# Agent attention with a top-1 mixture of experts: another path for the second phase's left rows, and earlier checks in the last batch

## The chip, the cores and the metric

The kernel runs on one core of one Trainium2 chip. The metric is the device time of one execution in microseconds. Three runs of the kernel before took 730.01, 725.21 and 724.99 us, a median of 725.21 us.

## The reference

Four batches of 11456 tokens with 128 channels pass an attention through 49 agents, and the rows that come out pass a mixture of 8 experts, of which each row takes the one with the largest logit.

```python
a2k = sm(agents, k)                 # softmax over the tokens
agent_v = a2k @ v
x = sm(q, agents) @ agent_v         # 45824 rows of 128
e_idx = argmax(x @ w_gate)
h = maximum(x[mask] @ w1[e], 0)     # for each expert e, mask = rows that chose e
out[mask] = gate_w * eom * (h @ w2[e])
```

`gate_w` is the softmax probability of the chosen expert and `eom` the sigmoid of its output gate.

## The kernel before

For each batch the kernel averages `v` under the agents' weights and takes the expert that this average favours, the "dominant" one. Nearly all rows choose it, so the main stream computes all rows of a batch with that expert's weights, folded down to the agents. Each batch has 12 units of up to 1024 tokens (90 columns of 128 in all); a unit has two tiles of up to 512 columns, which `mm1` (line 1521) and `mm2` (1547) multiply.

A unit of queries goes through `q_rest` (1306: maximum and difference on VectorE, into a tile `ef` of a ring of FRONT = 6), `weights` (1321: exponentials, then the transposed copy `x1`, which stands in one of 13 places: 7 LARGE, which also take the loads of q, k and v, and 6 SMALL), `route` (1347) and `gate` (1374: the gate values, and a store of `ef` to a table in HBM). The list `rests` notes for each unit how far it is: 1 with `x1` there, 2 within `gate`, 3 with `ef` stored. `roomy` (1299) lets the units of the last batch run 9 ahead of the main stream. `gate` spawns `signs` (1428) at priority 1: for each of the 90 columns one matmul `ck` and one ScalarE activation `cx` whose sum tells whether the fold could be wrong for a row. When all units are checked, `q_tail` (1452) makes on VectorE a table of 128 x 8 x 90 running counts of the rows that must be computed again, the "left rows", stores it, and writes its totals to `tot`.

The left rows are collected by expert into tiles of 128, in two phases: batches 0 and 1 have 14 tiles, batches 2 and 3 have 4 (`PHASES`, line 38). `left_prepare` (1947) waits until the phase's batches are counted and the phase before is prepared, and runs

- `left_table` (1665): which expert and which ranks belong to which tile;
- `left_index` (1736) for each set of tiles (phase 0: 4, 4, 4 and 2 tiles, whose names end in 0s, 4s, 8s and 12s; phase 1: one set of 4): which partition and which column of it holds each row, by comparisons on VectorE, one gather per tile from the counts (`big<-cumd`), some fifteen small steps, and one gather per tile from the stored exponentials (`big<-efd`), all gathers on GpSimd's queue. The set 12s starts only when 8 tiles are stored.

`left_static` (1975) then computes the 18 tiles in order: `left_load` (1863) fetches the expert's two matrices, 512 KB each, into one of two homes (`lw` and `lws` in the trace), `left_front` (1894) rebuilds the rows (`let`, `lx`), `left_back` (1911) multiplies them by both matrices (`lh`, then `ly`, 8 matmuls in four-byte numbers each), and `left_scatter` (2008) writes the rows out through GpSimd's queue. Homes are loaded again only when the tile that used them is done.

No order is written out by hand. All these parts are Python generators; `spawn(generator, priority)` hands them to a planner (`tick`, 527, and `Clock`, 67) that keeps a modelled time of every engine and emits an instruction when its operands should be ready, lower priority numbers first. TensorE's stream has slots for them between the main matmuls. Every engine works its queue in the order of emission, so an instruction that was emitted too early holds up what stands behind it. Nearly all instructions are recorded in one helper, so their line in the profile is 248; they are told apart by tile.

Of the kernel before, what the change touches and what calls it, by code (L numbers as in the profile page):

```python
# [17 lines left out]
P = 128  # L18
B, N, C, A, E, F = 4, 11456, 128, 49, 8, 1024
A2 = 50  # L20
# [38 lines left out]
K_W = K_GA2 + NG_  # L59
# [238 lines left out]
def agent_attention_top1_moe(ctx, tc, qT, kT, v, aT, wg, wo, w1, w2, cst, sides, slots, out):  # L298
# [95 lines left out]
    ticol = kc[:, K_TI:K_TI + 2]  # L394
    own = kc[:, K_OWN:K_OWN + 1]
# [45 lines left out]
    ls = cp.tile([2 * E, P + 2], F32, name="ls")  # L441
# [170 lines left out]
    def place(item, k, shape, dt=F32):  # L612
        kind, b, u = item
        t = ld.tile([P] + shape, dt, name=f"{kind}{b}_{u}_ld", tag=f"ld{k}", bufs=1)
        places[k] = [False, t.name]
        held[item] = k
        return t
# [27 lines left out]

    def loads():
        for n, item in enumerate(ITEMS):
            while n >= FIRST_ITEMS and (picking[0] or not X1):
                yield None
            while not vacant():  # L650
                yield None
            yield from load(item)
            if n == 1:
                load_constants()

# [640 lines left out]
    rests = []  # L1296
    squared = set()
# [8 lines left out]
    def q_rest(b, u, s, mark):  # L1306
        base, pp, nt = UNITS[u]
        me = len(rests)
        rests.append(0)
        while me >= FRONT and rests[me - FRONT] < 3 or me > 1 and not state.get(0, {}).get("w"):  # L1310
            yield None
        sv = s[0:pp, 0:nt * A2].rearrange("p (t a) -> p t a", a=A2)[:, :, 0:A]
        m = wk.tile([P, 8], F32, name=f"qm{b}_{u}", tag="qm", bufs=3)
        yield from DVE.q.tensor_reduce(m[0:pp, 0:nt], sv, axis=AX.X, op=ALU.max)
        ef = wk.tile([P, 8, A2], F32, name=f"ef{b}_{u}", tag="ef", bufs=FRONT)
        ev = ef[0:pp, 0:nt, 0:A]
        yield from DVE.q.tensor_tensor(ev, sv, m[0:pp, 0:nt].unsqueeze(2).broadcast_to([pp, nt, A]), op=ALU.subtract)
        release(mark)
        spawn(weights(b, u, me, ef, ev), 1)

    def weights(b, u, me, ef, ev):
# [23 lines left out]
        spawn(route(b, u, me, x1, ef), 0.3)  # L1345

# [27 lines left out]
    def gate(b, u, me, x1, ef, L, lm, d256, rr, tl):  # L1374
# [9 lines left out]
        vs = vss[b % 2][:, 8 * u:8 * u + nt]  # L1384
        spawn(signs(b, u, me, x1, vs), 1)
# [37 lines left out]
        if u == NU - 1:  # L1423
            spawn(q_tail(b), 0.5)
# [26 lines left out]

    def q_tail(b):

        while NU * b + NU - 1 not in signed or "thr" not in state[b]:
            yield None
        e2, dq, vs = e2s[b % 2], dqs[b % 2], vss[b % 2]
        yield from DVE.q.scalar_tensor_tensor(e2, e2, state[b]["thr"], dq, op0=ALU.mult, op1=ALU.is_gt)
        yield from DVE.q.scalar_tensor_tensor(e2, vs, 0.0, e2, op0=ALU.is_gt, op1=ALU.max)
        c0 = wk.tile([P, E, NCOL], F32, name=f"cum{b}", tag="cum", bufs=1)
        f = c0.rearrange("p e t -> p t e")  # L1460
        yield from DVE.q.tensor_tensor(f, e2.unsqueeze(2).broadcast_to([P, NCOL, E]),
                                       state[b]["ndom"].unsqueeze(1).broadcast_to([P, NCOL, E]), op=ALU.max)
        yield from DVE.q.tensor_tensor(f, f, oht[b % 2], op=ALU.mult)
# [192 lines left out]
    lp = ctx.enter_context(tc.tile_pool(name="lp", bufs=1))  # L1656
    NSTM = max(x[2] for x in PHASES)
# [7 lines left out]
    def left_table(ph):  # L1665
# [30 lines left out]
        ppt = lt(f"pptsb{ph}", [P], f"_{ph}", [P])  # L1696
# [165 lines left out]

    def left_load(ph, ti, k, nm, home=None):
# [4 lines left out]
        if home == "sel":  # L1868
# [78 lines left out]
    def left_prepare(ph):  # L1947
# [4 lines left out]
        if ph == 0:  # L1952
            yield from SY.q.dma_start(ls, sides)
        yield from left_table(ph)
# [20 lines left out]
    def left_static():  # L1975
# [5 lines left out]
        def fronts():  # L1981
            for i, (ph, k) in enumerate(todo):
                while (ph, k) not in known or i > finished[0] + 1 or busy["own"] and (busy["sel"] or planning()):
                    yield None
                home = "sel" if busy["own"] else "own"
                busy[home] = True
                w1t, w2t = yield from left_load(ph, *known[ph, k], f"{ph}_{k}", home)
# [8 lines left out]

        spawn(fronts(), 0.3)
# [40 lines left out]
    spawn(loads(), -1)  # L2038
    spawn(gate_norm(), 5)
# [34 lines left out]
def _consts():  # L2074
# [8 lines left out]
    k[:, K_TI:K_TI + 2] = i[:, None] + 128 * np.arange(2)  # L2083
    k[:, K_OWN] = i < 2 * A
# [7 lines left out]
def _sides():  # L2092
# [3 lines left out]
    return np.concatenate([sign * (np.arange(P)[None] + 0.5), g % E, sign], axis=1).astype(np.float32)  # L2096
# [36 lines left out]
```

## Time and profile before

| what | us |
|---|---|
| median of three runs | 725.21 |
| profiled execution, its own time | 728.79 |
| its span, first to last instruction | 727.0 |
| TensorE busy in the span | 641.8 |
| VectorE, ScalarE, GpSimd busy | 506.2, 498.1, 277.3 |

The profiled execution is 1.8 us longer than its span and 3.6 us longer than the median. Instants below are microseconds from the start of the span. TensorE's mean granted clock is 0.973 of full speed. A row of the timeline gives start, duration, engine, operation, output and inputs; in brackets stands how long the engine was idle before it and what released it.

### The profile page before, as it was taken

Reading aid. Unit: us, or ns where it says so; the run is one execution under the profiler, and the core shown is the slowest. Engines: PE = TensorE matmul, PEld = TensorE weight load, DVE = VectorE, ACT = ScalarE, POOL = GpSimd, SP = SyncE. Lnnn points to the kernel's source line nnn. Section 1 sums busy time; section 2 is a strip of 40 time slices with the busy share of each in tenths; the row PEclk is TensorE's granted clock in tenths of the full one; section 3 lists DMA queues with packets and bytes.
Section 4 is the critical chain, followed back from the end, with each engine's and each line's share of the span. In section 5 each row is a group of like instructions: output and inputs, shape, how many; then the busy total and the mean of one; then the engine's idle time right before and its main releaser. Section 6 shows DMA issues by size and latency. Waiting matters only on the chain. (4 is left out here: it accounts for less than half of the span.)

```text
span 727.0 us, 27442 instructions
## 1 busy us (share of the span) xinstructions
PE 641.8 (88%) x10693; PEld 533.2 (73%) x10693; DVE 506.2 (70%) x1744; ACT 498.1 (69%) x1724; POOL 277.3 (38%) x569
## 2 busy tenths in 40 slices
PE   9998989898998898799999888969999999996174
PEld 7788877687775787588777577858887789786064
DVE  1677868786878965789888889777687866544300
ACT  2325568996878886687888789666788878772021
POOL 2011247822132677223257623433455354122231
PEclk9999999999999999999999999999999999999678
DMA  8788697799566579976759995536563743455221
GB/s 304 279 250 276 194 272 257 220 224 285 167 187 195 145 230 307 270 220 164 223 157 286 255 259 162 151 96 197 144 196 114 206 163 135 163 182 150 97 76 58
DMA packets 103110, 143.81 MB, mean 198 GB/s; under 512 B 60188, under 2 KB 68541, under 8 KB 102976
## 3 DMA queue, kind: packets, MB, share of 16 engines
q1 hardware_dynamic: 101248, 139.95, 65.0%
q0 software_dynamic: 1728, 2.06, 1.3%
q8 instruction: 85, 1.39, 0.8%
q14 instruction: 49, 0.40, 0.2%
HBM read 95.23 MB, written 35.43 MB: 180 GB/s over the span
## 5 line engine op out<-in xcount | busy, mean ns | idle before, releaser
L248 PE MATMUL y<-vv,hh 128*128 128x128 f16 (+1 forms) x1440 | 159.5, 220 | 1.7 <-issue 1.7
L248 ACT ACTIVATE cx<-ck 128x256 f16<-128x256 f32 x360 | 139.6, 388 | 26.2 <-PE ck L248 20.5
L248 PE MATMUL y<-vv,hl 128*128 128x128 f16 x720 | 139.8, 220 | 0.0
L248 DVE SCALAR_TENSOR_TENSOR hl<-h,hh 128x512 f16<-128x512 f32 (+1 forms) x184 | 117.9, 669 | 17.9 <-ACT hh L248 16.1
L248 PEld LDWEIGHTS <-x_ld 128*128 128x128 f16 (+1 forms) x1440 | 97.9, 99 | 41.7 <-issue 24.0
L248 PEld LDWEIGHTS <-hh 128*128 128x128 f16 (+1 forms) x1440 | 113.8, 99 | 6.6 <-issue 3.2
L248 ACT ACTIVATE hh<-h 128x512 f16<-128x512 f32 (+1 forms) x184 | 101.5, 591 | 15.1 <-PE h L248 14.4
L248 PE MATMUL y<-gw,x_ld 128*128 128x128 f16 x720 | 79.8, 220 | 4.4 <-ACT cx L248 2.2
L248 PE MATMUL ck<-wc,x_ld 128*128 128x256 f16 x360 | 72.6, 274 | 7.3 <-ACT cx L248 2.7
L248 PEld LDWEIGHTS <-hl 128*128 128x128 f16 x720 | 73.5, 102 | 2.9 <-issue 1.6
L248 ACT ACTIVATION_READ_ACCUMULATOR cx<-ck 128x1 f32 x360 | 74.5, 207 | 0.0
L248 PE MATMUL h<-x_ld,w 128*128 128x512 f16 (+1 forms) x184 | 69.1, 376 | 4.9 <-DMA x_ld<-e 3.4
L248 DVE TENSOR_TENSOR os<-y,smt 128x256 f32<-128x256 f32 (+1 forms) x92 | 38.1, 414 | 49.1 <-ACT os L248 43.5
L248 POOL TENSOR_TENSOR e<-ef,e 128x392 f16<-128x392 f32 (+1 forms) x48 | 43.1, 898 | 69.5 <-ACT e L248 68.6
L248 PE MATMUL h<-x_ld,wr 128*128 128x512 f16 (+1 forms) x184 | 68.6, 373 | 0.0
L248 ACT ACTIVATE os<-y,smt 128x128 f32<-128x128 f32 x180 | 56.7, 367 | 11.4 <-PE y L248 9.5
L248 PE MATMUL warm<-apart 128*128 128x256 f16 (+1 forms) x286 | 47.6, 290 | 11.7 <-DVE hl L248 3.8
L248 PE MATMUL ks<-at,k_ld 128*32 128x50 f32 (+1 forms) x2024 | 51.7, 218 | 3.0 <-issue 3.0
L248 PEld LDWEIGHTS ks<-at,k_ld 128*32 128x32 f32 (+1 forms) x2024 | 43.9, 123 | 12.3 <-issue 5.7
L248 PEld LDWEIGHTS <-apart 128*128 128x128 f16 x382 | 40.7, 123 | 15.6 <-issue 9.0
L248 ACT COPY S<-ks 128x400 f32<-128x400 f32 (+1 forms) x48 | 22.5, 469 | 38.8 <-PE ks L248 38.5
L248 PE MATMUL qs<-at,q_ld 128*32 128x50 f32 (+1 forms) x2504 | 46.8, 211 | 2.2 <-ACT hgc L248 1.1
(345 smaller groups left out, 1477.2 us busy)
## 6 DMA issues: line engine op xcount, KB each, us to landing
v_ld<-v SPq DMA_DIRECT2D x44, 512.0 KB
q_ld<-qT SPq DMA_DIRECT2D x44, 512.0 KB
out<-os SPq DMA_DIRECT2D x88, 256.0 KB
k_ld<-kT SPq DMA_DIRECT2D x43, 512.0 KB
lw<-w SPq DMA_DIRECT2D x18, 512.0 KB
lws<-w SPq DMA_DIRECT2D x18, 512.0 KB
efd<-ef SPq DMA_DIRECT2D x44, 200.0 KB
w1t<-w SPq DMA_DIRECT2D x4, 512.0 KB
```

The source lines that it names most:

```text
L248: return getattr(self.eng, op)(*a, **k)
```

## The change

Last batch: its units may run 12 ahead of the main stream instead of 9; an `ef` that finds no room in the ring takes a LARGE place, as long as three stay free while loads are still to come; `signs` is spawned in `weights`, right behind the transposed copy, at priority 0.25 instead of 1 and no longer in `gate`; and `q_tail` treats columns 0 to 79 when the first ten units are through and the other ten columns after that, with one scan over all at the end.

Second phase: `left_table` and `left_index` give way to `late_table`, `late_index` and `late_end`. The tables are read as sums of steps (a comparison, a product and a sum over nine), rows are compared in PSUM without a copy to SBUF, the gathers of the four tiles are worked on one by one, and the tables that only the overflow loop reads are made last. `late_weights` fetches the matrices of the four tiles as soon as the experts are known, into free LARGE places, and into the two old homes once phase 0 is done. The table of partition sums has one buffer for both phases. A few columns of constants are added, and four small memsets at the start.

```diff
-        while me >= FRONT and rests[me - FRONT] < 3 or me > 1 and not state.get(0, {}).get("w"):
-            yield None
+        while me > 1 and not state.get(0, {}).get("w"):
+            yield None
+        while True:
+            if len(fronts_) < FRONT or rests[fronts_[-FRONT]] > 2:
+                at_ = None
+                break
+            at_ = first_place(0, LARGE, 0 if loaded[0] else 3) if b == B - 1 else None
+            if at_ is not None:
+                break
+            yield None
+            fronts_.append(me)
+            ef = wk.tile([P, 8, A2], F32, name=f"ef{b}_{u}", tag="ef", bufs=FRONT)
+        else:
+            ef = place(("ef", b, u), at_[1], [1024])[:, 0:8 * A2].rearrange("p (t a) -> p t a", a=A2)
...
+        if b == B - 1:
+            spawn(signs(b, u, me, x1, vss[b % 2][:, 8 * u:8 * u + nt]), 0.25)
...
-        vs = vss[b % 2][:, 8 * u:8 * u + nt]
-        spawn(signs(b, u, me, x1, vs), 1)
+        if b < B - 1:
+            spawn(signs(b, u, me, x1, vss[b % 2][:, 8 * u:8 * u + nt]), 1)
...
-        if u == NU - 1:
+        if ("ef", b, u) in held:
+            scored(("ef", b, u))
+        if u == (CUT // 8 if b == B - 1 else NU) - 1:
             spawn(q_tail(b), 0.5)
...
+    CUT = 80
...
-        while NU * b + NU - 1 not in signed or "thr" not in state[b]:
-            yield None
...
+        c0 = None
+        for lo, hi in ((0, CUT), (CUT, NCOL)) if b == B - 1 else ((0, NCOL),):
+            us = range(NU if hi == NCOL else CUT // 8)
+            while not all(NU * b + u in signed and rests[NU * b + u:NU * b + u + 1] == [3] for u in us) or "thr" not in state[b]:
+                yield None
+            if c0 is None:
...
+            yield from DVE.q.tensor_tensor(f, e2.unsqueeze(2).broadcast_to([P, hi - lo, E]),
...
+            yield from DVE.q.tensor_tensor(f, f, oht[b % 2][:, lo:hi], op=ALU.mult)
...
-            while kind == "q" and not roomy(NU * b + u, 9 if b == B - 1 else AHEAD):
+            while kind == "q" and not roomy(NU * b + u, 12 if b == B - 1 else AHEAD):
...
+    def left_steps(n9, W, first, step, prod, o):
...
+        yield from DVE.q.tensor_tensor(step, n9.unsqueeze(1).broadcast_to([P, n, 9]),
+                                       first.unsqueeze(2).broadcast_to([P, n, 9]), op=ALU.is_le)
+        yield from DVE.q.tensor_tensor(prod, step.unsqueeze(2).broadcast_to([P, n, 4, 9]),
+                                       W.unsqueeze(1).broadcast_to([P, n, 4, 9]), op=ALU.mult)
+        yield from DVE.q.tensor_reduce(o, prod, axis=AX.X, op=ALU.add)
+
+    def late_table(ph, big):
...
+        yield from PE.q.matmul(cn_[:, 0:ng], ones, tt_, start=True, stop=True)
+        yield from DVE.q.tensor_copy(c10[:, 0, 1:9], cn_[:, 0:E])
+        yield from DVE.q.tensor_tensor(c10[:, 1, 1:9], cn_[:, E:2 * E], c10[:, 0, 1:9], op=ALU.add)
+        release(mark)
+        ti_ = lt("t1i", [E], f"_{ph}", [E], I32)
+        yield from DVE.q.tensor_scalar(ti_, c10[:, 1, 1:9], 127.0, None, op0=ALU.add)
+        yield from DVE.q.tensor_scalar(ti_, ti_, -128, None, op0=ALU.bitwise_and)
+        yield from DVE.q.tensor_copy(W[:, 3, 1:9], ti_)
+        yield from DVE.q.tensor_tensor(W[:, 1:3, :], c10[:, :, 1:10], c10[:, :, 0:9], op=ALU.subtract)
+        yield from DVE.q.tensor_tensor_scan(n9[:, 1:9], ones[:, 0:E], W[:, 3, 1:9], 0.0, op0=ALU.mult, op1=ALU.add)
+        yield from DVE.q.tensor_tensor(W[:, 1:3, :], W[:, 1:3, :], W[:, 3, :].unsqueeze(1).broadcast_to([P, 2, 9]), op=ALU.add)
...
+        PE.matmul(pt_[0:ng, 0:P], tt_, tri, start=True, stop=False)
+        PE.matmul(pt_[0:ng, 0:P], tt_, idf, start=False, stop=True)
...
+        yield from ACT.q.copy(ppt[0:ng], pt_[0:ng, 0:P])
...
+        yield from left_steps(n9, W, kc[:, K_KK:K_KK + n], big[:, 0:9 * n].rearrange("p (n e) -> p n e", e=9),
...
+        yield from DVE.q.tensor_scalar(nd, tb[0:ng, :, 0], expert, BIG, op0=ALU.not_equal, op1=ALU.mult)
+        yield from DVE.q.scalar_tensor_tensor(low, tb[0:ng, :, 1], sign, ls[:, P + 2:P + 2 + n], op0=ALU.mult, op1=ALU.subtract)
+        yield from DVE.q.tensor_tensor(nd, nd, low, op=ALU.add)
...
+        yield from DVE.q.tensor_scalar(ti, tb[:, :, 0], float(E - 1), None, op0=ALU.min)
...
+    def left_places(nm, n, tb, rk, bi, r, base, b2):
...
+        yield from DVE.q.tensor_tensor(bi[:, :, 1:3], rk.unsqueeze(2).broadcast_to([P, n, 2]), tb[:, :, 1:3], op=ALU.is_ge)
+        yield from DVE.q.tensor_tensor(r, rk, start, op=ALU.subtract)
...
+        yield from DVE.q.tensor_scalar(bi[:, :, 0], bt, -1.0, 1.0, op0=ALU.mult, op1=ALU.add)
...
+    def late_end(ph):
...
+        yield from left_steps(n9, W, ticol8, f[:, 0:9 * kr].rearrange("p (n e) -> p n e", e=9),
...
+        yield from POOL.q.memset(tt, 0.0)
...
+    def late_index(ph, nm, big, oa_, got):
...
+        yield from DVE.q.tensor_tensor(c[0:ng], side.unsqueeze(1).broadcast_to([ng, n, P]),
+                                       nd.unsqueeze(2).broadcast_to([ng, n, P]), op=ALU.is_ge)
...
+        for k in range(n):
+            yield from PE.q.matmul(t[:, k * P:(k + 1) * P], c[0:ng, k, :], ppt[0:ng], start=True, stop=True)
...
+        yield from left_places(nm, n, tb, kc[:, K_RK:K_RK + n], bi, r, base, b2)
...
+        yield from DVE.q.tensor_tensor(c, pb, r.unsqueeze(2).broadcast_to([P, n, P]), op=ALU.is_le)
+        pst = col("pst")
+        yield from DVE.q.tensor_reduce(pst, c, axis=AX.X, op=ALU.add)
+        ru = col("ru", U32)
+        yield from DVE.q.tensor_tensor(ru, pst, base, op=ALU.add)
...
+        for k in range(2):
+            yield from gather(k)
+        yield from DVE.q.tensor_tensor(c, c, pb, op=ALU.mult)
+        yield from DVE.q.tensor_reduce(ppx, c, axis=AX.X, op=ALU.max)
...
+        yield from DVE.q.memset(ef, 0.0)
+        yield from DVE.q.scalar_tensor_tensor(b2, pst, 8.0, b2, op0=ALU.mult, op1=ALU.add)
+        for k in range(n):
+            if k + 2 < n:
+                yield from gather(k + 2)
+            yield from pause(landed[k] + 200.0 - clk.now())
+            s_, x = slice(k, k + 1), cr[:, k:k + 1, :]
+            yield from DVE.q.tensor_scalar(x[:, 0], x[:, 0], ppx[:, s_], None, op0=ALU.is_le)
+            yield from DVE.q.tensor_reduce(c7[:, s_], x[:, :, 7:NCOL:8], axis=AX.X, op=ALU.add)
+            yield from DVE.q.scalar_tensor_tensor(f[:, s_], x[:, :, 87], -6.0, pst[:, s_], op0=ALU.mult, op1=ALU.mult)
+            yield from DVE.q.tensor_reduce(cc[:, s_], x, axis=AX.X, op=ALU.add)
+            yield from DVE.q.tensor_tensor(f[:, s_], f[:, s_], b2[:, s_], op=ALU.add)
...
+            yield from DVE.q.tensor_tensor(tu[:, s_], f[:, s_], cc[:, s_], op=ALU.add)
+            yield "POOL", [tu], [], 0
+            POOL.indirect_dma_start(out=ef[:, k, :], out_offset=None, in_=efd[ph],
...
+            got(k, clk.ready[big.name] + 200.0, None, tu, tg, ef, oa, xt, two)
+            yield from DVE.q.scalar_tensor_tensor(tg[:, s_], f[:, s_], float(b0 * N), cc[:, s_], op0=ALU.add, op1=ALU.add)
...
+        if home not in (None, "own", "sel"):
+            w1t, w2t = (place((*home, j), first_place(0, LARGE)[1], [F]) for j in range(2))
...
+        if ph == len(PHASES) - 1:
+            while sum(x[0] for x in places[:LARGE]) < 2:
...
+            big, oa_ = (place((x, ph, 0), first_place(0, LARGE)[1], [1024]) for x in ("lb", "lo"))
+            yield from late_table(ph, big)
+            averaged[ph] = yield from left_averages(ph, f"{ph}")
...
+            yield from late_index(ph, f"s{ph}_0", big, oa_, got)
+            yield from late_end(ph)
+            prepared[0] = ph + 1
+            return
...
-                while (ph, k) not in known or i > finished[0] + 1 or busy["own"] and (busy["sel"] or planning()):
+                while (ph, k) not in known or i > finished[0] + 1 or ph < last_ and busy["own"] and (busy["sel"] or planning()):
+                    yield None
+                while ph == last_ and (ph, k) not in weights_:
                     yield None
...
+                if (ph, k) in weights_:
+                    home, w1t, w2t = weights_.pop((ph, k))
...
+        def late_weights():
+            for k in range(PHASES[last_][2]):
+                while (last_, k) not in known:
+                    yield None
+                while True:
+                    if len([j for j in range(LARGE) if places[j][0]]) > 1:
+                        home = ("left", last_, k)
+                    elif finished[0] >= len(todo) - PHASES[last_][2] and not (busy["own"] and busy["sel"]):
+                        home = "sel" if busy["own"] else "own"
+                    else:
+                        yield None
+                        continue
```

## Rows read from the trace of the kernel before

**Rows 1.** Stretches: busy PE, PEld, DVE, ACT, POOL (instructions), clock, DMA share, GB/s

```profile
600.00:620.00 20.00, 20.00 (x234) 17.97 (x234) 12.36 (x59) 15.85 (x64) 9.05 (x21) 1.00 0.43 146
...
680.00:700.00 20.00, 5.52 (x23) 4.96 (x24) 4.25 (x20) 1.55 (x4) 8.06 (x9) 0.50 0.07 13
700.00:727.00 27.00, 15.30 (x119) 14.20 (x118) 0.00 (x0) 6.27 (x17) 3.97 (x4) 0.88 0.26 87
```

**Rows 2.** Timeline, the four tiles of phase 1 to the last instruction

```profile
693.77 0.42 PE L248 MATMUL let<-kc,big 128*98 128x128 f32 x1 [19.26 <-DVE big L248]
...
695.70 3.78 PE L248 MATMUL lh<-lxs,lw 128*128 128x128 f32 x16 [0.35 <-ACT lxs L248]
...
708.46 2.05 PE L248 MATMUL lh<-lxs,lw 128*128 128x128 f32 x16 [0.35 <-ACT lxs L248]
...
713.03 2.05 PE L248 MATMUL lh<-lxs,lws 128*128 128x128 f32 x16 [0.39 <-ACT lxs L248]
...
717.67 0.98 POOL L248 DMA_INDIRECT out<-big,ltg_0s  x1 [2.33 <-ACT big L248]
```

**Rows 3.** Timeline, phase 1's table and index from the counts to the first tile

```profile
656.80 0.40 PE L248 MATMUL pexc<-tot,kc 128*128 128x16 f32 x2 [1.48 <-DVE tot L248]
...
665.15 0.17 DVE L248 TENSOR_REDUCE tt<-cm 128x2 f32<-128x16 f32 x1 [3.44 <-POOL tt L248]
...
668.56 0.19 DVE L248 COPY tbs<-tbs 128x32 f32<-128x32 f32 x1 [1.22 <-PE tbs L248]
...
674.55 0.59 ACT L248 COPY big<-pbs 128x512 f32<-128x512 f32 x1 [0.27 <-PE pbs L248]
...
675.16 0.69 DVE L248 TENSOR_TENSOR big<-big,lrs 128x512 f32<-128x512 f32 x1 [3.91 <-ACT big L248]
...
678.73 0.17 DVE L248 CAST lrus<-lrgs 128x4 uint32<-128x4 f32 x1
679.68 1.05 POOL L248 DMA_INDIRECT big<-cumd,lrus  x1 [4.15 <-issue]
...
683.66 1.00 POOL L248 DMA_INDIRECT big<-cumd,lrus  x1 [0.30 <-issue]
...
686.97 0.53 DVE L248 TENSOR_TENSOR big<-big,lppxs 128x360 f32<-128x360 f32 x1 [8.07 <-DMA big<-cumd,lrus]
...
690.38 0.17 DVE L248 CAST ltg_0s<-lts 128x4 uint32<-128x4 f32 x1
690.89 1.00 POOL L248 DMA_INDIRECT big<-efd,ltu_0s  x1 [5.95 <-issue]
...
693.40 0.26 DVE L248 TENSOR_TENSOR big<-big,ltwo_0s 128x98 f32<-128x98 f32 x1 [2.85 <-DMA big<-efd,ltu_0s]
```

**Rows 4.** Timeline, phase 0's last set, `q_tail`'s scan and phase 0's last tiles

```profile
643.14 1.00 POOL L248 DMA_INDIRECT big<-cumd,lrus  x1 [0.30 <-issue]
...
648.18 0.34 DVE L248 TENSOR_TENSOR big<-big,lppxs 128x180 f32<-128x180 f32 x1
...
648.63 2.05 PE L248 MATMUL lh<-lxs,lw 128*128 128x128 f32 x16 [0.57 <-ACT lxs L248]
...
653.90 1.65 DVE L248 TENSOR_TENSOR_SCAN cum<-apart,cum 128x720 f32<-128x720 f16 x1
...
656.50 0.17 DVE L248 CAST ltu_12s<-lts 128x2 uint32<-128x2 f32 x1
...
668.82 2.05 PE L248 MATMUL lh<-lxs,lws 128*128 128x128 f32 x16 [0.30 <-ACT lxs L248]
...
674.55 0.98 POOL L248 DMA_INDIRECT out<-big,ltu_12s  x1 [4.67 <-DMA lw<-w]
```

**Rows 5.** The checks' ScalarE work (tile `cx`, two instructions a check) in two stretches

```profile
600.00:620.00 20.00, 7.64 (x32) 1.00 0.43 146
...
640.00:660.00 20.00, 5.69 (x24) 1.00 0.56 166
```

**Rows 6.** Timeline of SyncE's queue, the last unit's store of `ef`

```profile
623.67 0.33 SPq L248 DMA_DIRECT2D efd<-ef  x1
```

More of the change, by code (lines that the diff above doesn't have):

```diff
@@ L58 @@
 K_GA2 = K_GAM + NG_
-K_W = K_GA2 + NG_
+K_TI8 = K_GA2 + NG_
+K_KK = K_TI8 + 2
+K_RK = K_KK + 4
+K_W = K_RK + 4
 LANDS = 1500.0
@@ L644, in load @@
         parts[item] = t
+    loaded = [False]
     def loads():
@@ L1656, in agent_attention_top1_moe @@
     lp = ctx.enter_context(tc.tile_pool(name="lp", bufs=1))
+    lw = {m: cp.tile([P, *k], F32, name=m) for m, k in (("c10", (2, 10)), ("w9", (4, 9)), ("n9", (9,)))}
     NSTM = max(x[2] for x in PHASES)
@@ new lines, in left_places @@
+    def left_places(nm, n, tb, rk, bi, r, base, b2):
+        u, start = tb[:, :, 1], tb[:, :, 3]
+        bt, inv = bi[:, :, 1], bi[:, :, 2]
+        yield from DVE.q.tensor_tensor(bi[:, :, 1:3], rk.unsqueeze(2).broadcast_to([P, n, 2]), tb[:, :, 1:3], op=ALU.is_ge)
+        yield from DVE.q.tensor_tensor(r, rk, start, op=ALU.subtract)
+        yield from DVE.q.tensor_tensor(b2, u, start, op=ALU.subtract)
+        yield from DVE.q.tensor_tensor(b2, b2, bt, op=ALU.mult)
+        yield from DVE.q.tensor_tensor(r, r, b2, op=ALU.subtract)
+        yield from DVE.q.tensor_scalar(base, tb[:, :, 0], float(E - 1), 128.0, op0=ALU.min, op1=ALU.mult)
+        yield from DVE.q.scalar_tensor_tensor(base, bt, 128.0 * E, base, op0=ALU.mult, op1=ALU.add)
+        yield from DVE.q.tensor_scalar(b2, bt, float(N), None, op0=ALU.mult)
+        yield from DVE.q.scalar_tensor_tensor(b2, inv, BIG, b2, op0=ALU.mult, op1=ALU.add)
+        yield from DVE.q.tensor_scalar(bi[:, :, 0], bt, -1.0, 1.0, op0=ALU.mult, op1=ALU.add)
@@ new lines, in late_end @@
+    def late_end(ph):
+        b0, nb, nst, rows = PHASES[ph]
+        kr = rows // P
+        W, n9 = lw["w9"], lw["n9"]
+        f = wk.tile([P, E, NCOL], F32, name=f"steps{ph}", tag="cum", bufs=1).rearrange("p e t -> p (e t)")
+        t4 = f[:, 45 * kr:49 * kr].rearrange("p (n c) -> p n c", c=4)
+        tt = lt(f"tt{ph}", [kr, 8], f"_{ph}", [kr, 8])
+        yield from left_steps(n9, W, ticol8, f[:, 0:9 * kr].rearrange("p (n e) -> p n e", e=9),
+                              f[:, 9 * kr:45 * kr].rearrange("p (n c e) -> p n c e", c=4, e=9), t4)
+        yield from POOL.q.memset(tt, 0.0)
+        yield from DVE.q.tensor_scalar(tt[:, :, 0], t4[:, :, 0], float(E - 1), None, op0=ALU.min)
+        yield from DVE.q.tensor_tensor(tt[:, :, 1], ticol8, t4[:, :, 3], op=ALU.subtract)
+        yield from DVE.q.tensor_tensor(tt[:, :, 2], t4[:, :, 2], t4[:, :, 3], op=ALU.subtract)
+        yield from DVE.q.tensor_tensor(tt[:, :, 4], t4[:, :, 1], t4[:, :, 3], op=ALU.subtract)
+        tti = lt("tti", [kr, 8], f"_{ph}", [kr, 8], I32)
+        yield from DVE.q.tensor_copy(tti, tt)
+        yield from SY.q.dma_start(ttd[ph].rearrange("(k p) c -> p k c", p=P), tt)
+        yield from SY.q.dma_start(ttid[ph].rearrange("(k p) c -> p k c", p=P), tti)
+        yield from DVE.q.tensor_scalar(nti[ph], n9[:, 8:9], 1.0 / 128.0, None, op0=ALU.mult)
+        yield from DVE.q.tensor_scalar(over[:, ph:ph + 1], n9[:, 8:9], 128.0 * nst, None, op0=ALU.is_gt)
@@ L1995, in fronts @@
                 ops[ph, k] = home, (xs, w1t, w2t)
+        last_ = len(PHASES) - 1
+        weights_ = {}
+        def late_weights():
[7 more added lines that the diff above has]
+                        home = "sel" if busy["own"] else "own"
+                    else:
+                        yield None
+                        continue
+                    break
+                busy[home] = True
+                weights_[last_, k] = home, *(yield from left_load(last_, *known[last_, k], f"{last_}_{k}", home))
+        spawn(late_weights(), 0.3)
         spawn(fronts(), 0.3)
@@ L2038, in agent_attention_top1_moe @@
     spawn(loads(), -1)
+    POOL.memset(lw["c10"], 0.0)
+    POOL.memset(lw["w9"], 1.0)
+    POOL.memset(lw["w9"][:, :, 0:1], 0.0)
+    POOL.memset(lw["n9"], 0.0)
     spawn(gate_norm(), 5)
```

96 lines of the change are left out of this document (79 added, 17 removed).

## The prediction

> **What bounds the kernel now.** The stretches at the end are read first [rows 1]. From 600 to 620 us TensorE has no idle time at all, so up to there its work sets the pace; the reader is to see how that ends: from 680 to 700 it works 5.52 of 20 us, and at a granted clock of 0.50, which is the lower of its two levels. The timeline of the tail says what it waits for. The first tile of phase 1 starts with the transpose at 693.77, after 19.26 us without a matmul, released by VectorE [rows 2]; the last scatter starts at 717.67, and the span ends 9.3 us behind its start. Backwards from 693.77 there is one chain of small steps: gathers, comparisons, a table, and in front of it a matmul at 656.80 that waited 1.48 us for the totals `tot` [rows 3]. The totals wait in turn for the last check and for the scan of `q_tail` at 653.90 [rows 4]. So the end is a chain of latencies, 60.9 us from 656.80 to 717.67, and no engine is the bound in it.
>
> **The change part by part.** All is reckoned along that chain: when the table starts, how long from there to the first `lh`, how long the four tiles take.
>
> *Start of the table, 656.80 before.* Two conditions hold it: the counts of batch 3, and phase 0 being prepared, that is, the gathers of its last set 12s issued. The first moves up. There are 16 checks in 600 to 620 and 12 behind 640 (half the instructions) [rows 5], with their units' transposed copies standing ready, because they have the lower priority; the last unit's `ef` is stored at 623.67 [rows 6]. Asked for at priority 0.25, they should be through soon after 625, and the totals with them: the last ten columns cost a ninth of `q_tail`'s wide operations, the scan stays (1.65 us). That takes the second condition into the lead. Set 12s compares at 648.18 and has its rows at 656.50 [rows 4], 8.3 us for a chain of steps that took 3.6 us in phase 1's set (686.97 to 690.55) [rows 3]; the rest are `q_tail`'s pieces between them. Without them it has its rows at 648.2 + 3.6 = 651.8, and I start the table there: 5.0 us earlier. Bounds: 645, if set 12s is also helped by the missing checks, and 657, no gain. The checks themselves are the same instructions at the same price, so the main stream's sum of work stays; their 0.48 us of ScalarE each (7.64 over 16) [rows 5] move into 520 to 600. There ScalarE has room: in 600 to 620, with 16 checks, it was busy 15.85 of 20 us while TensorE never idled [rows 1]. I cost that at nothing; bounds from -3 to +10 us on the main stream's end.
>
> *From the table to the first `lh`, 38.9 us before (656.80 to 695.70).* Up to the cast that ends the row numbers it takes 22.1 (to 678.90) [rows 3], with a stall of 3.44 for a memset behind a scatter on GpSimd and 3.91 for ScalarE's copy of the PSUM tile. After: a matmul and a copy, 0.7; some fifteen small steps at 0.19 each (as (690.55 - 686.97 - 2 x 0.53) / 13 gives), 3.0 with the slightly wider products; the wide comparison, about 0.7 as its like at 675.16; ten small steps, 2.0, with the four matmuls under them; a wide comparison, a sum and an addition, 1.6. Sum 8.0, so 14.1 less. Next the gathers. Before, 0.8 to the first issue, four at a pitch of 1.33 and 2.3 from the end of the last (684.66) to the comparison at 686.97: 8.1. After, the first tile waits for its own gather alone: 0.8 + 1.05 + 2.3 = 4.1. The second wide product is off the path, in this wait. Then seven small steps, 1.4, where fifteen took 3.6; then as before 0.3 to the issue, 1.0, and 1.5 from its end (691.89) to VectorE at 693.40, and 2.3 to `lh`: 5.2. Sum 8.0 + 4.1 + 1.4 + 5.2 = 18.7.
>
> Undisturbed, that is 20.2 us less. It will not be undisturbed: the old chain ran its second half on an empty core, the new one runs beside phase 0's last four tiles. Its matmuls stand in TensorE's queue between `lh` and `ly`, and its eight gathers stand in GpSimd's queue between up to four scatters of a microsecond, each of which waits there for its tile, as the one at 674.55 did for 4.67 us [rows 4]. I add 4 us, with bounds 0 and 10: 22.7 us to the first `lh`. Fetching the matrices early removes no wait in front of the first `lh`, which waited 0.35 us and for ScalarE [rows 2]; it puts 2 MB beside the gathers. Gathers next to traffic show up to 4.0 us from issue to use (643.14 + 1.00 to 648.18 [rows 4]) against 2.3 in the quiet stretch; this 1.7 twice is within the 4 us.
>
> On that the Trainium skill speaks against the change: "DMA: Bandwidth & Descriptors", section SWDGE vs HWDGE vs iDMA, says that the software queue of GpSimd and the hardware queues feed different internal queues of the same DMA engines, and that each engine takes them in turn. By it the gathers would be slowed by the early matrices every time; the row of 4.0 us does not contradict. Charged in full beside the 4 us, it would make 3.4 us more, 706.4 in place of 703.0.
>
> *The core is not free earlier than phase 0 lets it.* Four of its tiles start behind the main stream, at 648.63 and up to 668.82 [rows 4]. Their pitch with everything at hand is 4.57 us (708.46 to 713.03 [rows 2]), so they could end at 648.6 + 4 x 4.6 = 667; set 12s, 5 us earlier, does not hold them longer than that. The first `lh` of phase 1 comes at the later of 667 and 651.8 + 22.7 = 674.5.
>
> *The four tiles, 21.97 us before (695.70 to 717.67).* With matrices at hand: three pitches of 4.57 and 4.64 from the last `lh` to the scatter, 18.4. Before, the first two took 12.76 instead of 9.14, 3.6 us more, with the first `lh` at 3.78 us instead of 2.05 on the low clock. TensorE would idle from 667 to about 673, so I keep half of the 3.6, bounds 0 and 3.6: 20.2 us, scatter at 694.7.
>
> The trace shows the clock at 0.50 in 680 to 700, with TensorE idle for most of that stretch [rows 1, 2]. The Trainium skill, "TensorE: Matmul & The Clock Gate", Part 1, says the same from the other side: throttled is the default, and activity lifts it. [...]
>
> *Sum.* The scatter moves from 717.67 to 694.7, 23.0 us. What follows stays (9.3). By the profiled execution, 728.79 - 23.0 = 705.8; that execution lay 3.6 above the median, and 725.21 - 23.0 = 702.2 is the same on the median. I round up to 703 for `late_end` and its memset, which stand in the queues ahead of later tiles.
>
> **Rivals.**
>
> *TensorE is the bound to the end.* If the chain is through before phase 0's tiles are, phase 1 follows at 667 without a gap: scatter at 667 + 18.4 = 685.4, 32.3 us gained, 693. For it speaks that the counts may be ready by 630; against it that set 12s alone held the table, and that phase 0's tiles before did not keep the best pitch.
>
> *GpSimd's queue takes the place of the chain.* If the table starts no earlier (657) and the gathers stand behind phase 0's scatters (10 us), the first `lh` comes at 657 + 28.7 = 685.7, on a cold clock, and the scatter at 707.7: 10 us gained, 715. The waits of 3.44 and 4.67 us speak for it; against it, that those scatters are four.
>
> *The early fetch holds phase 0's own matrices back.* SyncE works in order; it waits for the new tile numbers and then issues 2 MB ahead of what the last tiles of phase 0 want. If phase 0 ends at 685 instead of 674.5 and the clock falls, little is left: about 720, within 1%. Against it: in 600 to 620, with stores, matrices and gathers in flight, the DMA engines were busy 0.43 of the time [rows 1].
>
> *Slower: the checks stall the main stream.* Place: 520 to 600, where the checks now stand ahead of the evacuations of `h` on ScalarE and hold PSUM banks. Price: at worst the whole 0.48 us for each of 90 checks, 43 us, because TensorE's idle time there is lost for good. It decides from 23 us on, 48 checks wholly exposed; in full it gives 725 + 20 = 745, at 35 us 737. Against it stands the stretch with 16 checks and no idle TensorE [rows 1, 5].
>
> **How the numbers follow.** The forecast, 698 to 709, gets 0.50; TensorE bound 0.20; GpSimd's queue 0.20; the early fetch 0.06; slower 0.04. The likeliest gives 703. From 692 to 716 the range holds the first three, with the ends of the unknown costs (645 and no disturbance; 657 and 10 us) in it. About 1%, 7.25 us, is what a measurement of this kernel can tell from no change: faster 0.90, same 0.06, slower 0.04.
>
> **What would show it.** Right: the last check before 635 and `tot` before 645; no idle time of 19 us in front of the first transpose of phase 1; less than 25 us from the table's matmul to the first `lh`; its first gather used before the fourth is issued; the four tiles at 4.6 us. Wrong: `tot` still waited for; GpSimd's gathers idle behind a scatter; the main stream's last `y` later than 650; phase 0's last tile after 680; a first `lh` of phase 1 near 3.8 us with a long gap would mean that the clock's full price stays.

## The result, and the profile after

The change runs in 703.79 us (median of four runs, 700.64 to 706.84) beside 726.88 us for the kernel before on the same chip (724.99 to 730.01): a ratio of 0.968, interval 0.962 to 0.974, or 23 us. Two repeats beside other kernels gave 0.973 (0.967 to 0.979) and 0.971 (0.967 to 0.976). The profiled execution took 706.84 us, its span 705.1; before, 728.79 and 727.0. (These are medians of four runs each; the 725.21 us above are that of the first three.)

First the stretches at the end (columns as in [rows 1]):

```profile
600.00:620.00 20.00, 20.00 (x227) 18.10 (x225) 13.97 (x56) 18.71 (x75) 9.52 (x19) 1.00 0.46 147
660.00:680.00 20.00, 14.01 (x88) 12.87 (x88) 9.12 (x51) 4.34 (x11) 9.08 (x9) 0.83 0.69 234
680.00:705.00 25.00, 14.58 (x130) 14.34 (x128) 1.17 (x10) 7.52 (x18) 5.09 (x6) 0.89 0.14 47
```

The empty stretch of [rows 1], 5.52 of 20 us at a clock of 0.50, is gone. TensorE works 14.0 of 20 us in 660 to 680, and the clock in the last 45 us is 0.83 and 0.89.

Then the checks (tile `cx` on ScalarE, two instructions each; columns: stretch, busy time, count, clock, DMA share, GB/s):

```profile
600.00:620.00 20.00, 9.68 (x40) 1.00 0.46 147
620.00:640.00 20.00, 0.97 (x4) 1.00 0.55 181
```

Where 24 instructions stood behind 640 [rows 5], four stand behind 620, and none behind 640. ScalarE has taken them at 18.71 of 20 us, and TensorE has no idle time beside it in 600 to 620.

The timeline of the chain, from the last store of `ef` to the last scatter:

```profile
625.82 0.33 SPq L251 DMA_DIRECT2D efd<-ef_ld  x1
...
635.26 0.16 DVE L251 COPY tot<-cum 128x8 f32<-128x8 f32 x1
...
650.39 0.17 DVE L251 CAST ltu_12s<-lts 128x2 uint32<-128x2 f32 x1
...
651.42 1.00 POOL L251 DMA_INDIRECT out<-big,ltu_8s  x1 [7.64 <-ACT big L251]
...
655.27 0.29 PE L251 MATMUL cnt<-tot,ones 128*128 128x16 f32 x2
...
662.63 0.16 DVE L251 TENSOR_TENSOR lrus<-lpsts,lrgs 128x4 uint32<-128x4 f32 x1
663.07 1.03 POOL L251 DMA_INDIRECT lb_ld<-cumd,lrus  x1 [4.82 <-DVE lrus L251]
...
669.38 0.27 DVE L251 TENSOR_SCALAR lb_ld<-lb_ld,lppxs 128x90 f32<-128x90 f32 x1 [4.84 <-DMA lb_ld<-cumd,lrus]
...
670.36 2.02 PE L251 MATMUL lh<-lxs,lws 128*128 128x128 f32 x16 [2.66 <-DMA lws<-w]
...
672.62 1.00 POOL L251 DMA_INDIRECT lb_ld<-cumd,lrus  x1 [0.30 <-issue]
...
674.95 3.13 PE L251 MATMUL ly<-lws,lh 128*128 128x128 f32 x16
...
678.86 1.18 PE L251 MATMUL lh<-lxs,left_ld 128*128 128x128 f32 x8 [0.35 <-ACT lxs L251]
...
682.89 1.06 PE L251 MATMUL lh<-lxs,left_ld 128*128 128x128 f32 x8
...
695.26 0.96 POOL L251 DMA_INDIRECT out<-lo_ld,ltg_0s  x1 [2.73 <-ACT lo_ld L251]
```

Read it against [rows 2 to 4]. The counts are there at 635.26, and nobody waits for them: the table's first product stands at 655.27, 1.5 us before its old place. From there to the first `lh` of phase 1 it is 23.6 us in place of 38.9, and from that to the last scatter 16.4 in place of 22.0. The scatter moved from 717.67 to 695.26, 22.4 us; 9.8 us follow it, where 9.3 did.

These instants hang on one more: the main stream's last `y`. Before, then in the change:

```profile
646.76 0.22 PE L248 MATMUL y<-vv,hl 128*96 128x128 f16 x1
```

```profile
652.08 0.22 PE L251 MATMUL y<-vv,hl 128*96 128x128 f16 x1
```

In two more profiles of the change, taken beside E5 and E9 below, it stands at 645.00 and 651.30, and what follows moves with it: the table's product follows it by 3.2 us in all three, where 10.0 had passed before. So profiles are best compared by distances, in us:

| kernel | last `y` at | product to first `lh` | product to last scatter | last `y` to last scatter |
|---|---|---|---|---|
| before | 646.76 | 38.9 | 60.9 | 70.9 |
| the change, three profiles | 652.08, 645.00, 651.30 | 23.6, 22.2, 22.3 | 40.0, 39.6, 39.4 | 43.2, 42.8, 42.6 |
| E1, short path alone | 649.38 | 28.0 | 45.9 | 56.0 |
| E2, checks alone | 662.30 | 35.9 | 57.2 | 61.4 |
| E3, no early fetch | 661.52 | 19.9 | 41.1 | 45.3 |
| E4, fetch held back | 657.60 | 26.5 | 44.2 | 48.4 |

### The profile page after: what moved, and what is told of

Read it like the earlier page. It is cut to its first block, busy times and chain, and to the rows that moved or that the text cites. A ratio compares the mean times of both kernels' runs of the same rounds, so it can differ in the third digit from the quotient of the medians.

```text
span 705.1 us, 27438 instructions
## 1 busy us (share of the span) xinstructions
PE 643.6 (91%) x10692; PEld 537.1 (76%) x10692; DVE 507.3 (72%) x1763; ACT 495.8 (70%) x1723; POOL 280.0 (40%) x572
## 5 line engine op out<-in xcount | busy, mean ns | idle before, releaser
L251 PEld LDWEIGHTS <-x_ld 128*128 128x128 f16 x1440 | 98.2, 100 | 43.0 <-issue 24.1
L251 POOL TENSOR_TENSOR e<-ef,e 128x392 f16<-128x392 f32 (+1 forms) x43 | 39.1, 909 | 63.5 <-ACT e L251 62.6
L251 PE MATMUL warm<-apart 128*128 128x256 f16 (+1 forms) x286 | 50.4, 306 | 9.5 <-DVE hl L251 3.8
L251 PEld LDWEIGHTS qs<-at,q_ld 128*32 128x32 f32 (+1 forms) x2504 | 40.7, 116 | 10.5 <-issue 3.3
```

What stands on the lines that cost most here:

```text
L251: return getattr(self.eng, op)(*a, **k)
```

## The experiments

The first four kernels shared one chip, on which the kernel before took 730.32 us; the later ones had 724.23, 724.03 and 725.13 us. Across chips only the ratios are compared.

**E1 and E2, the two halves alone.** E1 has the short path and the early fetch, with the last batch's checks, fronts and `q_tail` as before. E2 has the new checks and the old second phase. The central lines of the two edits:

```
E1: ...
    -        if b == B - 1:
    -            spawn(signs(b, u, me, x1, vss[b % 2][:, 8 * u:8 * u + nt]), 0.25)
    ...
    -        if b < B - 1:
    +        if True:
                 spawn(signs(b, u, me, x1, vss[b % 2][:, 8 * u:8 * u + nt]), 1)
    ...
E2: ...
    -            yield from late_table(ph, big)
    ...
    -        spawn(late_weights(), 0.3)
    ...
```

> The change with the last batch's checks, fronts and counting as they were before; only the second phase's new path stays. Theory A (the counts and the counting's pieces between set 12s's steps held the table): the totals come again at about 656, the table's first matmul at 657 instead of 655.3, and set 12s has its rows at 655 to 657 instead of 650.4; last scatter 697 to 701, time 705 to 710. Rival B (the shorter path alone makes the gain, since set 12s and phase 0's tiles hold the table anyway): within 1 us of the change, 703 to 705. Rival C (the checks are worth most of it): above 715.

> The change with the second phase's old table, old index and matrices fetched in turn; only the earlier checks stay. Theory A: totals at about 635, set 12s's rows at 650 to 652, table's first matmul 652 to 655 instead of 656.8, and from there the old 38.9 us to the first lh and 22 us to the last scatter; time 720 to 725, 2 to 6 us less than before. Rival B: the chain of phase 0's last set holds the table wherever the counts are, 726 to 728, no difference. Rival C: most of the gain, below 712.

E1: 718.14 us, ratio 0.981 (0.977 to 0.986). E2: 729.43 us, 0.998 (0.995 to 1.001). E1's timeline:

```profile
659.10 0.17 DVE L251 CAST ltu_12s<-lts 128x2 uint32<-128x2 f32 x1
659.18 0.17 DVE L251 COPY tot<-cum 128x8 f32<-128x8 f32 x1
...
659.40 0.39 PE L251 MATMUL cnt<-tot,ones 128*128 128x16 f32 x2 [1.47 <-DVE tot L251]
...
687.36 1.92 PE L251 MATMUL lh<-lxs,left_ld 128*128 128x128 f32 x8
...
705.33 0.98 POOL L251 DMA_INDIRECT out<-lo_ld,ltg_0s  x1 [2.71 <-ACT lo_ld L251]
```

E2's:

```profile
645.14 0.17 DVE L251 COPY tot<-cum 128x8 f32<-128x8 f32 x1
...
662.30 0.22 PE L251 MATMUL y<-vv,hl 128*96 128x128 f16 x1
...
666.53 0.29 PE L251 MATMUL pexc<-tot,kc 128*128 128x16 f32 x2
...
700.45 0.42 PE L251 MATMUL let<-kc,big 128*98 128x128 f32 x1 [19.28 <-DVE big L251]
...
702.38 3.79 PE L251 MATMUL lh<-lxs,lw 128*128 128x128 f32 x16 [0.36 <-ACT lxs L251]
```

In E1 the table waits for the totals again, as in [rows 3], and set 12s's row numbers take 8.3 us from their comparison at 650.80, with `q_tail`'s pieces between them; in the change 2.6 (from 647.78). In E2 the totals are 21 us ahead of the table, and the old path behind it keeps its 19 us without a matmul and its first `lh` at 3.79 us; at 35.9 us it is little shorter than the 38.9 of before. So the short path is worth some 14 us alone, the checks at most 4 (0.25% by the median), and the change 20 to 23: about 5 us come only from the two together, a figure about as wide as its intervals. The profiles agree with it: E1's path from the product to the last scatter is 6 us longer than the change's, with its table's matmuls spread between phase 0's tiles (666.63 to 671.88).

The expectations were stated for the first chip. By its ratio E1 would take 713 us there, between theory A and rival C, so none of the three was met; for E2 it was rival B, no difference. But E2's profile says more than that the checks are worth nothing. From the last `y` to the last scatter it has 61.4 us in place of 70.9; what it gained there it lost in front of it, with a last `y` at 662.30. Some of that is this execution, 734.91 us where E2's median was 729.43, and some the chip, 730.32 us for the kernel before. Part of the rest can be read off: before, and in E1, four tiles of phase 0 start behind the main stream and twelve to fifteen checks run behind 640; in the change, E2, E3 and E4 three tiles start there and no check runs. A tile's two products take 1.9 us each and a check's `ck` about 0.2, so that some 6 us of TensorE's work, by this estimate, have moved in front of the last `y`.

**E3 and E4, the early fetch.** E3 fetches phase 1's matrices in their turn, as phase 0's are. E4 holds them until the pair of phase 0's last tile is issued.

```
E3: ...
    -        spawn(late_weights(), 0.3)
    ...
E4: ...
    -                while (last_, k) not in known:
    +                while (last_, k) not in known or issued[0] < len(todo) - PHASES[last_][2]:
    ...
```

> The change without the early fetch of the second phase's matrices: each tile's pair is fetched into one of the two old homes when that is free. Theory A (the 2 MB beside the gathers slow them and hold back phase 0's last pair, but they make the tiles follow at 3.9 us): first gather used less than 3.8 us after its issue ends instead of 5.3, last lh of phase 0 at 668.5 or before instead of 670.4 and not released by a DMA; the four tiles at 4.6 to 5.5 us again; time 703 to 709. Rival B (the gathers' wait has another cause, say the third gather): 5.3 us stay. Rival C (the early fetch is a plain loss): below 701.

> The change with the early fetch held until phase 0's last pair of matrices has been issued. Theory A (the early pairs ahead of it in SyncE's queue held that pair back): last lh of phase 0 at 667.5 to 668.7 instead of 670.4, released by ScalarE's lxs instead of a DMA; first lh of phase 1 at 676 to 677.5 instead of 678.9, where the gathers' chain then holds it; time 701 to 703, 1 to 2.5 us less than the change. Rival B (the gathers' chain held phase 1 all along): no difference, 703 to 705. Rival C (the matrices come too late for phase 1): above 705.

E3: 713.36 us, 0.972 (0.967 to 0.977). E4: 714.66 us, 0.974 (0.970 to 0.979). The change's three ratios are 0.968, 0.973 and 0.971, so neither can be told from it. E3's timeline:

```profile
673.50 1.03 POOL L251 DMA_INDIRECT lb_ld<-cumd,lrus  x1 [4.81 <-DVE lrus L251]
...
677.22 0.27 DVE L251 TENSOR_SCALAR lb_ld<-lb_ld,lppxs 128x90 f32<-128x90 f32 x1 [2.24 <-DMA lb_ld<-cumd,lrus]
...
685.58 3.79 PE L251 MATMUL lh<-lxs,lw 128*128 128x128 f32 x16 [0.35 <-ACT lxs L251]
...
692.17 2.05 PE L251 MATMUL lh<-lxs,lws 128*128 128x128 f32 x16 [0.39 <-ACT lxs L251]
...
697.58 2.05 PE L251 MATMUL lh<-lxs,lw 128*128 128x128 f32 x16 [0.35 <-ACT lxs L251]
```

The fetch gives with one hand and takes with the other. Without it the first gather is used 2.7 us after its issue has ended (674.53 to 677.22), not 5.3, and the first `lh` comes 19.9 us behind the table's product at 665.70, not 23.6. But the tiles then stand 6.6, 5.4 and 4.6 us apart, and from the first `lh` to the last scatter (706.79) it is 21.2 us, not 16.4. (The first of these pitches also holds an `lh` of 3.79 us, at the low clock.) In E4 the pair of phase 0's last tile is in time, yet a scatter of phase 0 takes the place of that wait, in front of the gather of `ef`:

```profile
674.43 2.05 PE L251 MATMUL lh<-lxs,lws 128*128 128x128 f32 x16 [1.17 <-ACT lxs L251]
...
680.60 0.99 POOL L251 DMA_INDIRECT out<-big,ltu_12s  x1 [5.09 <-DMA lw<-w]
681.89 1.05 POOL L251 DMA_INDIRECT lb_ld<-efd,ltu_0s  x1 [0.30 <-issue]
```

**E5 and E6, the scatters out of the way.** Phase 0's last six scatters are held until the last gather of phase 1 is issued; E6 also has E4's edit. A repeat of the change ran beside them. The edit of E5:

```
+            while stored[0] >= 8 and (len(PHASES) - 1, 3) not in ready:
+                yield None
```

> The change as it stands, again, beside the kernels of this call. Expected as before: a ratio to the kernel before of 0.962 to 0.974. If it comes out near 0.98, the runs without the early fetch (0.972) and with the fetch held back (0.974) would have lost nothing against it.

> The change, with phase 0's last six scatters held back until the last gather of phase 1's table rows is issued; all else as in the change. Theory (GpSimd's queue is in order, so a scatter that waits for its tile holds the gathers behind it: 7.64 us in front of set 12s's efd gathers in the changed kernel's profile): the efd gathers of set 12s start with their row numbers, phase 0's last tiles and then phase 1's come 3 to 6 us sooner, 2 to 5 us off the time of the change on this chip. Rival (phase 0's last tiles are held by their own matrices and phase 1's gathers by the transfers of the early fetch, so that the queue only takes the place of another wait): no more than 1 us.

> The same hold on the scatters, and phase 1's matrices not fetched before the pair of phase 0's last tile is issued. Theory (two waits, the queue and the transfers, each hidden behind the other; with the fetch alone held back, a scatter stood 5.09 us in front of the gathers): now both go, the first gather lands 2.5 to 3 us after its issue rather than 5 to 6, and the time is 3 to 8 us under that of the change on this chip. Rival (the later matrices cost at the first tiles what the gathers gain): within 2 us of the kernel that holds back the scatters alone.

The repeat: 703.58 us, 0.973 (0.967 to 0.979). E5: 716.79 us, 0.988 (0.982 to 0.995). E6: 716.19 us, 0.987 (0.980 to 0.993). Both theories fell: 13 us were lost, none gained, and E6's first gather of counts was used 5.9 us behind its issue, not 2.5 to 3. E5's timeline:

```profile
690.63 2.05 PE L251 MATMUL ly<-lws,lh 128*128 128x128 f32 x16
...
694.19 0.98 POOL L251 DMA_INDIRECT out<-big,ltu_12s  x1 [2.04 <-ACTq L2288]
...
703.27 0.98 POOL L251 DMA_INDIRECT out<-lo_ld,ltg_0s  x1 [2.03 <-DMA out<-lo_ld,ltg_0s]
706.22 0.98 POOL L251 DMA_INDIRECT out<-lo_ld,ltg_0s  x1 [1.96 <-DMA out<-lo_ld,ltg_0s]
```

TensorE's last product ends at 692.7, and five more scatters follow, 3.0 us apart: each waits 2 us, and for three of the five, the last two among them, the trace names the landing of the one before. Ten of them cannot be put behind the gathers for nothing. And the 7.64 us for which a scatter stood in front of set 12s's gathers had hidden little: the first of these is issued 1.2 us behind its row numbers in E5 and 2.5 in the repeat (649.23 - 648.00 and 645.81 - 643.30).

**E7 and E8, the table at once.** The table of phase 1 starts as soon as the counts are there, beside set 12s's index (with places of their own for some small tiles); E8 also has E4's edit.

```
...
-        while counted[0] < b0 + nb or ph > prepared[0]:
+        while counted[0] < b0 + nb or ph > prepared[0] + 1:
...
```

> The change, with phase 1's table started as soon as the last batch's counts are there, beside set 12s's index instead of behind it (some small tiles get places of their own for that). Theory (with the counts out of the way, what sets the table's start is that set 12s's row numbers have to be finished first: in the repeated change the counts were there at 628.2, set 12s's row numbers at 643.4, the table's first product at 648.2): the table's first product comes 8 to 15 us sooner, phase 1's first gather 5 to 12 us sooner, its first lh right behind phase 0's last tile, and the time is 5 to 10 us under that of the change, a ratio of 0.958 to 0.966. Rival (phase 0's last tiles, held by GpSimd's queue and their own matrices, set the end anyway, and the earlier table only delays set 12s on VectorE): within 3 us of the change, 0.968 to 0.977.

> The same early table, with phase 1's matrices not fetched before the pair of phase 0's last tile is issued. Theory (the fetch slows the gathers and the matrices of phase 0): the first rows of counts land 2.5 to 3.5 us behind their gather's issue, phase 0's last two tiles do not wait for their matrices, and the time is 1 to 4 us under that of the early table alone. Rival (the fetch costs as much as it gives): within 1.5 us of it.

E7: 703.74 us, 0.971 (0.962 to 0.980). E8: 703.63 us, 0.969 (0.960 to 0.977). No difference from the change, so in the time both rivals hold. E7's timeline:

```profile
632.68 0.35 PE L251 MATMUL cnt<-tot,ones 128*128 128x16 f32 x2
...
651.21 0.22 PE L251 MATMUL y<-vv,hl 128*96 128x128 f16 x1
...
654.39 0.16 DVE L251 TENSOR_TENSOR lrus<-lpsts,lrgs 128x4 uint32<-128x4 f32 x1
...
656.88 1.02 POOL L251 DMA_INDIRECT lb_ld<-cumd,lrus  x1 [0.31 <-issue]
...
674.29 1.06 PE L251 MATMUL lh<-lxs,left_ld 128*128 128x128 f32 x8
```

The profile of the change whose last `y` stands at the same instant is the one taken beside E9 (its product at 654.49 and its first `lh` at 676.82 are shown there):

```profile
651.30 0.22 PE L251 MATMUL y<-vv,hl 128*96 128x128 f16 x1
...
661.85 0.16 DVE L251 TENSOR_TENSOR lrus<-lpsts,lrgs 128x4 uint32<-128x4 f32 x1
662.28 1.03 POOL L251 DMA_INDIRECT lb_ld<-cumd,lrus  x1 [4.82 <-DVE lrus L251]
```

The product moves up by 21.8 us, the row numbers by 7.5, the first gather by 5.4, the first `lh` and the last scatter (691.31 and 693.85) by 2.5, and the median by nothing that can be told. Up to the row numbers the path takes 7.5 us on the core that the main stream has left, and 21.9 beside the stream and set 12s, in whose queues on TensorE and VectorE its steps stand. What was still gained at the gather goes mostly at phase 0's last tile: phase 1's first `lh` stands right behind its `ly` (671.99, 2.47 us).

E8 held the fetch only until phase 0's last pair was issued, at 656.72, and the fetch followed at 658.13. So the two together fell on the first gather, whose issue ended at 659.71:

```profile
666.21 0.27 DVE L251 TENSOR_SCALAR lb_ld<-lb_ld,xppxs 128x90 f32<-128x90 f32 x1 [7.83 <-DMA lb_ld<-cumd,lrus]
```

It was used 6.5 us later, with the DMA engines at a share of 1.00 (660 to 665). In E7, whose fetch was issued at 642.25, long before the gather, it was used after 3.0 us (657.90 to 660.88).

**E9, the gathers together.** The four gathers of counts are issued one behind the other, and one comparison waits for all.

```
...
-            yield from pause(landed[k] + 200.0 - clk.now())
-            yield from DVE.q.tensor_scalar(x[:, 0], x[:, 0], ppx[:, s_], None, op0=ALU.is_le)
+        yield from pause(landed[-1] + 200.0 - clk.now())
+        yield from DVE.q.tensor_tensor(cr, cr, ppx.unsqueeze(2).broadcast_to([P, n, NCOL]), op=ALU.is_le)
...
```

> The change as it stands, once more, as the neighbour of the next kernel: a ratio to the kernel before of 0.966 to 0.976, as in its two runs so far.

> The change, with phase 1's four gathers of counts issued one behind the other and one comparison of all four behind the last of them, as the kernel before had it, so that the first tile no longer goes on with its own gather alone; all else as in the change. Theory (the term of the forecast that the first tile's own landing is enough): the first lh comes 2.6 us (two gathers more) to 6 us later; the four tiles then follow at 3.9 us as before, their matrices at hand, so the time is 2 to 6 us over that of the change. Rival (phase 0's last tile, held by its matrices, or the order of GpSimd's queue sets the first lh anyway): within 1.5 us.

The change beside it: 704.46 us, 0.971 (0.967 to 0.976). E9: 708.40 us, 0.977 (0.972 to 0.981), so 3.9 us more between the medians, though the intervals overlap. E9's timeline:

```profile
647.56 0.29 PE L251 MATMUL cnt<-tot,ones 128*128 128x16 f32 x2
...
665.77 0.53 DVE L251 TENSOR_TENSOR lb_ld<-lb_ld,lppxs 128x360 f32<-128x360 f32 x1 [8.73 <-DMA lb_ld<-cumd,lrus]
...
673.62 3.65 PE L251 MATMUL lh<-lxs,left_ld 128*128 128x128 f32 x16 [0.35 <-ACT lxs L251]
```

The timeline of the change beside it:

```profile
654.49 0.29 PE L251 MATMUL cnt<-tot,ones 128*128 128x16 f32 x2
...
668.14 0.27 DVE L251 TENSOR_SCALAR lb_ld<-lb_ld,lppxs 128x90 f32<-128x90 f32 x1 [4.39 <-DMA lb_ld<-cumd,lrus]
...
676.82 1.80 PE L251 MATMUL lh<-lxs,left_ld 128*128 128x128 f32 x8 [0.35 <-ACT lxs L251]
```

From the table's product to the first `lh` it is 26.1 us and 22.3, so 3.7 more; to the last scatter (692.85 and 693.85) it is 45.3 and 39.4, so 5.9 more. The other 2.2 us come in the tiles: in E9 the first `lh` takes 3.65 us, at the low clock, and the next one follows 6.2 us behind its start, not 3.9 as was expected. The term "the first tile waits for its own gather alone" is there, and it is worth about 4 us in the medians even beside the traffic.

## Why the prediction was right

The forecast was 703.0 us, the result 703.79; in the profiled executions 23.0 us were forecast and 21.95 came (728.79 to 706.84). The main mechanism, a shorter chain of latencies, is shown by E1 and by the distances: from the table's product to the last scatter 60.9 us before and 39.4 to 40.0 in three profiles of the change. Of the parts of that path only the gathers one by one (E9) and the early fetch (E3, E4) were tested alone; the smaller table and the steps saved on VectorE were not. That the sum came out within 1 us is luck in part: in this profile the table started 3.5 us later than forecast (in the two others at 648.18 and 654.49), and the four tiles took 3.8 us less.

*The checks.* Right: the last one is through at 621, the totals at 635, and TensorE's idle time did not grow; in 20 to 640 us it was busy 575.32 us before, 578.91 in the change and 579.52 in the repeat. The slower rival did not come. But the main stream's end was not left where it was: the last `y` came 5.3 us later in the change's profile, 1.8 sooner and 4.5 later in the two others, within the stated bounds of -3 to +10. More of phase 0's work stands in front of it, as E2 shows.

*Start of the table, forecast 651.8, measured 655.27.* The second condition took the lead, as forecast, and set 12s had its rows at 650.39, even a little sooner. What failed is the step "I start the table there". The product stands 4.9 us behind those row numbers, in all three profiles of the change (655.27 - 650.39, 648.18 - 643.30, 654.49 - 649.61). The condition, in the prediction's own words, was that set 12s's gathers be issued, and the step left the two issues out: a scatter first, then the gathers, the second of them done at 655.25. In TensorE's queue the product comes in the middle of the `ly` of a tile of phase 0. E7 shows that an earlier start was worth little in any case.

*Table to first `lh`, forecast 22.7, measured 23.6.* To the row numbers 7.5 us (8.0 forecast). To the comparison 6.6 (4.1), the gather beside 1 MB pairs. To the next row numbers 1.2 (1.4). To `lh` 8.3 (5.2), among it the `ly` of phase 0's last tile at 674.95, in the queue ahead, 3.13 us in place of 2.05. So 5.6 us of disturbance minus 0.7 elsewhere, where 4 were added. The forecast put the disturbance on TensorE's queue, GpSimd's scatters and the traffic; the rows show the first and the third, and E5 hardly any of the second.

On the traffic the Trainium skill, "DMA: Bandwidth & Descriptors", section SWDGE vs HWDGE vs iDMA, has the two kinds of queues share the engines in turn. E3 agrees in direction: without the fetch the first gather was used after 2.7 us, not 5.3, and the second after 1.5, not 2.2, so 3.3 us for both, where the forecast had weighed 3.4.

*Phase 0's end, forecast 667.* Its last tile began `lh` at 670.36, after 2.66 us for its own pair, issued behind the four early transfers, and its `ly` ended only at 678.1, because a transpose of phase 1 that waited for a gather stood in front of it in TensorE's queue. The first is the third rival's mechanism, at a small part of its price. That price, 720, was no sum: with the first `lh` at 685 and 21.97 us for the tiles, the scatter would stand at 707, which makes 714.5 us.

*The four tiles, forecast 20.2, measured 16.4.* The step that failed is the pitch, "4.57 with everything at hand". It is 3.9 (678.86, 682.89, and on to 690.73): transposes and `lx` of the next tile stand between the halves of the one before. That pitch needs the matrices there (E3: 6.6, 5.4 and 4.6) and the next tile's rows in time (E9, with the matrices there: 6.2, 4.6 and 4.0); the forecast counted the benefit of the early matrices only as a wait removed in front of the first `lh`. The half price of the low clock did not come in the tiles either: in 660 to 680 TensorE idled 6 of 20 us, and the half `lh` that follow took 1.06 to 1.18, the upper level. It was paid in front of them, in the `ly` of 3.13 us; in the profile beside E9 the first half `lh` took 1.80. And the 3.6 us were not all the clock's: the second pitch before, 5.4 us (703.05 to 708.46), had `lh` and `ly` at 2.05, so 0.8 of them came from the order of the steps.

For this the Trainium skill, "TensorE: Matmul & The Clock Gate", Part 1, has the throttle as the default and activity lift it. The rows agree: the `ly` at 674.95 started behind a gap of 2.42 us and took 3.13, and the half products behind it took 1.06 to 1.18.

*The signs named beforehand.* Those for right came, with the tiles at 3.9 us rather than 4.6. Two of those for wrong came as well. A scatter stood 7.64 us in front of set 12s's gathers, which E5 shows to have cost 1.3; and the last `y` was later than 650 in two of three profiles, which the shorter chain outweighed.

What stays open: how much of the last `y` at 657.6 to 662.3 in E2, E3 and E4 is the moved work, and how much the execution and the chip. The granted clock in 20 to 640 was 0.97 in E2 and E3 and 0.98 to 0.99 elsewhere, which has the right sign; no run separates these.

## What to carry to other kernels

When a chain of small steps sets the end, shorten the path behind the late event before moving the event: the short path alone gave 14 us, the earlier event alone next to nothing, and the two together about 5 more. Before a step is moved up, look at what stands in the in-order queues at its new place; of 21.8 us 2.5 were left at the first `lh`. A wait that the trace shows at 7.6 us may be worth 1.3, so count what is late next, and count the moved work at the end of the chain too. And compare two profiles by distances from a common event: the same kernel's last `y` stood at 645.00, 651.30 and 652.08.

## What the runs showed of the hardware

A gather's landing depends on what else is in flight: from the end of its issue to use it took 2.1 us in E1 with the DMA engines at a share of 0.35, 3.0 in E7 at 0.59, 2.7 in E3 at 0.80, 6.5 in E8 at 0.99, and 5.3 in the change, where it fell into these stretches (busy times as in [rows 1], then clock, DMA share, GB/s):

```profile
660.00:665.00 5.00, 5.00 (x29) 4.76 (x29) 3.85 (x14) 1.46 (x3) 1.63 (x2) 0.69 0.96 289
665.00:670.00 5.00, 2.14 (x16) 1.70 (x14) 0.58 (x4) 0.79 (x3) 2.40 (x3) 0.97 1.02 395
```

Scatters to one output that had nothing else to wait for went 3.0 us apart (E5), of which 1.0 is the issue. And the price of an idle stretch came behind it: TensorE was busy 2.96 of 5 us in 655 to 660 at a clock of 1.00, and all of 660 to 665 at 0.69, where an `lh` of phase 0 (661.08) took 3.09 us in place of 2.0. The main stream shows it too, busy 3.35 of 6 us in 280 to 286 at 1.00 and all of 286 to 292 at 0.72, but not each time: in E7 it was busy 3.32 of 6 us in the first of these stretches, and the second kept 1.00.
